# A Conformer block on one core: the eighth chunk's feed-forward products three and five without the columns of its empty rows, and its attention output projected by quarter matrices

## The chip, the cores and the metric

The kernel runs on one core of one Trainium2 chip. The metric is the device time of one execution in microseconds (us), lower is better.

## The reference

The input is `x`, two sequences of 4000 tokens with 512 features, in bfloat16. What is computed, cut to what matters here:

```
h  = layernorm(x);                x1 = x  + 0.5 * silu(h @ w_ff1_a) @ w_ff1_b      # 512 -> 2048 -> 512
h  = layernorm(x1);               x2 = x1 + softmax(h wq (h wk)' * scale) (h wv) @ w_o
h  = layernorm(x2);               conv module: h @ w_pw1, a * sigmoid(b), 3-tap depthwise,
                                  normalised over all tokens, silu(..) @ w_pw2;    x3 = x2 + that
h  = layernorm(x3);               x4 = x3 + 0.5 * silu(h @ w_ff2_a) @ w_ff2_b
return layernorm(x4)
```

## The kernel before

**Chunks and stages.** The tokens are cut into 16 chunks, eight per sequence (`TCB` = 8). A chunk has 512 tokens, four tiles of 128. 4000 is not a multiple of 512: chunk 7 and chunk 15 have 416 tokens, three tiles and 32 tokens over. The 32 tokens left over of both sequences lie in one tile, the fourth tile of chunk 7 (`SHARED`): rows 0 to 31 belong to chunk 7, rows 32 to 63 to chunk 15, rows 64 to 127 hold nothing. So this tile has 64 empty rows of 128. The feed-forward stages handle it with chunk 7; in attention chunk 7 has 416 queries. The stages follow one another: the first feed-forward stage over all chunks, attention over all chunks with the conv module beside it, the second feed-forward stage over all chunks.

**Products by quarters.** Most matrix products use Strassen's scheme in its Winograd form: the two factors are cut into quarters, sums and differences of quarters are formed on VectorE, and seven products of quarters take the place of eight. In `ff_quad` (line 1545) the tokens of a chunk are cut into two halves of two tiles, the features into two halves, the outputs into even and odd blocks. `product(k)` (line 1571) issues one of the seven: four matmuls, each 128x128 weights by a moving matrix of 256 columns, of tiles 0 and 1 or of tiles 2 and 3. Products 1, 2, 6, 7 and 4 go into columns of which tiles 0 and 1 need a part. Products 3 and 5 go only into outputs of tiles 2 and 3. Steps a to d of a quad issue products 1 and 5, 2 and 6, 7 and 3, and 4; between them ScalarE copies (`act(h...)`, `act(m5...)`) and VectorE adds (`plus`) carry sums from one PSUM bank to another. A chunk has four quads, and in between stand the units of the second matrix of the chunk before (`ff_units`).

**Attention output.** While chunk g's attention runs, chunk g-1's is finished in `units_late` (line 2406), step by step of g's 32 key tiles (`kt`). For a chunk of 512 tokens (`whole`) `project_quad` (line 2662) multiplies the 512x512 matrix `Wvo` in quarters: `out_sums` forms four sums of the attention output `OT` on VectorE, then follow 7 products of 4 matmuls with 256 columns, two copies on ScalarE, two additions and eight `residual` operations of 256 columns on VectorE; `project_fetch` brings two sums of weights back from DRAM at `kt` 2 and 6. For chunk 7 `project` (line 2615) does it plainly: for each tile four matmuls of 512 columns, and one `residual` of 512 columns. The weights (stationary) are there the tokens, so the fourth tile, with 32 tokens, uses 32 of the 128 columns of the array. As `Wvo` is kept with one of its quarters replaced by a difference, `project_fetch(3)` brings the true quarter at `kt` 3 and `project_fetch(2)` the difference at `kt` 15.

**The order of the work.** All operations of the program are recorded first, and the class `Plan` (line 112) then sets the order on every engine by a list schedule with its own estimates of durations, looking 60 us ahead, and lets some operations (`either`) go to ScalarE or VectorE. So a change in one place may move rows at others. Since all instructions are issued by the recorder, nearly all have line 95 (L95) in the profile; they are told apart by the tiles that they write and read. Names in the rows: `s` and `y` are the eight PSUM banks, `work`, `sums`, `keys`, `wff` and `xt` are five regions of SBUF, in which the same bytes have several uses over time.

Of the kernel before, what the change touches and what calls it, by code (L numbers as in the profile page):

```python
# [8 lines left out]
ALU = mybir.AluOpType  # L9
AF = mybir.ActivationFunctionType  # L10
# [5 lines left out]
TILE = 128  # L16
TPC = 4
CHUNK = TPC * TILE
N = B * T
TCB = -(-T // CHUNK)  # L20
# [4 lines left out]
SHARED = TCB * TPC - 1  # L25
HALF = 32
# [3 lines left out]
HC, HD, HF = CHUNK // 2, D // 2, FC // 2  # L30
# [11 lines left out]
def width(c):  # L42

    return CHUNK if c % TCB < TCB - 1 else T - (TCB - 1) * CHUNK


def token_tiles(c):

    return TPC if c < NCK - 1 else TPC - 1
# [6 lines left out]
def tile_rows(c, ti):  # L56

    if c % TCB < TCB - 1 or ti < TPC - 1:
        return slice(0, TILE)
    lo = c // TCB * HALF  # L60
    return slice(lo, lo + TAIL)
# [50 lines left out]
class Plan:  # L112
# [49 lines left out]
    @staticmethod  # L162
    def form(call):

        w = call.args[1]
        return tuple(32 if n <= 32 else 64 if n <= 64 else 128 for n in (w.shape[0], Plan.size(w)))
# [431 lines left out]
class Conformer:  # L598
# [564 lines left out]

    def ln_norm(self, c, sl, ti, out, b_out, eng, src=None):
        x, b_x = self.tokens(c, ti, src)
        ways = {"DVE": lambda e: e.tensor_scalar(out, x, self.mv[sl][:, ti, 0:1], self.rs[sl][:, ti:ti + 1], ALU.subtract, ALU.mult),
                "ACT": lambda e: e.activation(out, x, AF.Identity, bias=self.sh[sl][:, ti:ti + 1], scale=self.rs[sl][:, ti:ti + 1])}
        if eng == "any":
            self.S.either(ways, [b_x, self.b_mv[sl][ti], self.b_rs[sl][ti], self.b_sh[sl][ti]], [b_out])
        elif eng == "DVE":  # L1170
            self.S.op("DVE", ways["DVE"], reads=[b_x, self.b_mv[sl][ti], self.b_rs[sl][ti]], writes=[b_out])
        else:
            self.act(out, x, AF.Identity, [b_x, self.b_sh[sl][ti], self.b_rs[sl][ti]], [b_out],
                     bias=self.sh[sl][:, ti:ti + 1], scale=self.rs[sl][:, ti:ti + 1])

    def ln_middle(self, sl, two):
        self.S.op("POOL", lambda e: e.tensor_scalar(self.mv[sl][:, two, 0], self.st[sl][:, two, 0], -1.0 / D, None, ALU.mult),
# [40 lines left out]
    def ln_job(self, c, kind, eng="DVE", plan=(1, 1, 2, 2, 3, 4, 5, 5, 6, 6), slot=None, pe=None):  # L1218

        sl = self.nxt("ln", self.LN_SLOTS)  # L1220
        n = token_tiles(c) if slot is None else TPC
        stats, aggr, shift, norm = plan[0:4], plan[4], plan[5], plan[6:10]

        def tile(ti):
            if kind == "key":
                k = self.keys_home(c)
                self.ln_norm(c, sl, ti, self.h2[k][ti][0:TILE, :], self.b_h2[k][ti], eng)
                if ti == n - 1:
                    self.store_keys(c)
                return  # L1230
            if kind == "out":
                g = c * TPC + ti
                self.ln_norm(c, sl, ti, self.XT[g], self.bx[g], eng)
                if ti == n - 1:
                    self.store_out(c, 0, TPC)
                return
            s = slot if slot is not None else c % 2
            tok, b_tok = self.ltm[ti], self.b_ltm[ti]
            feat, b_feat = self.lnT[s][:, ti], self.b_lnT[s][ti]
            self.ln_norm(c, sl, ti, tok[0:TILE, :], b_tok, eng)  # L1240
            if pe:
                self.after(4, lambda: self.transpose_pe(ti, s, pe[ti], self.bank(4 + ti)))
            else:
                self.transpose(feat, tok, [b_tok], [b_feat])

        for ti in range(n):
            self.after(stats[ti], lambda ti=ti: self.ln_stats(c, sl, ti))
        self.after(aggr, lambda: self.ln_aggr(sl, n))
        if eng == "ACT":
            self.after(shift, lambda: self.ln_shift(sl, n))  # L1250
        for ti in range(n):
            self.after(norm[ti], lambda ti=ti: tile(ti))
# [292 lines left out]
    def ff_quad(self, c, q, st):  # L1545

        S, s = self.S, c % 2
# [7 lines left out]
        n, hw = (3, 3 * 64) if short else (2, HC)  # L1555
# [13 lines left out]

        def product(k, ps, b_ps, start=False):  # L1570
            form, b_f, mv, b_m = forms[k]
            for u in range(2):
                out = ps[:, u * hw:(u + 1) * hw].rearrange("p (t k) -> p t k", t=n)
                for j in range(2):
                    self.mm(out, form(2 * q + u, j), mv[j], start and u == 0 and j == 0, u == 1 and j == 1,
                            b_f + b_m, b_ps, skip_group_check=True)

        def silu(src, b_src, odd, half):
            if short:
# [826 lines left out]
    def units_late(self, o, kt):  # L2406

        if kt == 0:
            self.late_first(o)
        elif kt == 1:  # L2410
            self.late_second(o)
        elif kt < 7:
            m = (kt - 2) * 6
            self.late_third(o, 2, range(m, min(m + 6, PAIRS)))
            self.late_third(o, 4, {3: range(1), 4: range(1, 3), 5: range(3, 9), 6: range(9, PAIRS)}.get(kt, ()))
        whole = width(o) == CHUNK
        if kt == 2:
            self.ln_conv = self.nxt("ln", self.LN_SLOTS)
        if kt in (2, 6) and whole:
            self.project_fetch(kt // 4)  # L2420
        if kt in (3, 15) and not whole:
            self.project_fetch(3 if kt == 3 else 2)
        if kt == 14 and o == NCK - 2:
            self.project_fetch(3)
        if kt == 6 and whole:
            for q in range(2):
                self.S.op("POOL", lambda e, q=q: e.memset(self.OT[0:1, ONES // 128, q * HC:(q + 1) * HC], 0.0),
                          writes=[self.b_OTq[q][ONES // 128]])
            for n in range(4):
                self.out_sums(n)  # L2430
        for n in {7: (0,), 8: (1, 2), 9: (3,)}.get(kt, ()) if whole else ():
            self.project_quad(o, self.ln_conv, n)
        for ti in {9: (0, 1), 13: (2, 3)}.get(kt, ()) if not whole else ():
            self.project(o, ti, self.ln_conv)
            if ti % 2:
                self.ln_middle(self.ln_conv, slice(ti - 1, ti + 1))

    def units(self, g, kt):

# [222 lines left out]
    def project_quad(self, g, sl, step):  # L2662

        S, s = self.S, g % 2
# [4 lines left out]
        form = lambda m: (lambda u, j: self.OS[m][:, j, u * TILE:(u + 1) * TILE], lambda j: self.b_OS[m])  # L2669
        w = lambda k, e: (lambda j: self.Wvo[:, 2 * k + j, e * HD:(e + 1) * HD], self.b_Wvo)  # L2670
        t = lambda m: (lambda j: self.TW[m][:, j], self.b_TW[m])
# [13 lines left out]
        def residual(src, b_src, f, e):  # L2685
            for u in range(2):
                ti = 2 * f + u
                y, b_y = self.XT[g * TPC + ti][:, e * HD:(e + 1) * HD], self.bx[g * TPC + ti]
                S.op("DVE", lambda eng, y=y, u=u, ti=ti: eng.scalar_tensor_tensor(
                    out=y, in0=src[:, u * HD:(u + 1) * HD], scalar=self.rl[s][:, ti:ti + 1], in1=y, op0=ALU.mult, op1=ALU.add,  # L2690
                    accum_out=self.st[sl][:, ti, 2 * e:2 * e + 1]),
                    reads=[b_src, self.b_rl[s], b_y], writes=[b_y, self.b_st[sl][ti]])

        if step == 0:
            product(1, c, b_c, True)
            n = width(g - 1)
            if n < CHUNK:
                self.mm(h[:, n:], self.Wvo[:, 0, 0:128], self.Wvo[:, 0, 0:CHUNK - n], False, True, [self.b_Wvo], b_h,
                        skip_group_check=True)
            self.act(h[:, :], c[:, :], AF.Copy, [b_c], [b_h])  # L2700
            product(5, x, b_x, True)
            self.act(m5, x[:, :], AF.Copy, [b_x], [b_m5])
        elif step == 1:
            product(6, h, b_h)
            plus(x[:, :], b_x)
            product(2, c, b_c)
            residual(c, b_c, 0, 0)
        elif step == 2:
            product(7, h, b_h)
            plus(m5, b_m5)  # L2710
            product(3, x, b_x)
            residual(x, b_x, 0, 1)
            residual(m5, b_m5, 1, 1)
        else:
            product(4, h, b_h)
            residual(h, b_h, 1, 0)
            for k in range(2):
                two = slice(2 * k, 2 * k + 2)
                S.op("POOL", lambda e, two=two: e.tensor_tensor(out=self.st[sl][:, two, 0], in0=self.st[sl][:, two, 0],
                                                                in1=self.st[sl][:, two, 2], op=ALU.add),  # L2720
                     reads=self.b_st[sl][two], writes=self.b_st[sl][two])
                self.ln_middle(sl, two)
# [814 lines left out]
```

## Time and profile before

| what | value |
|---|---|
| median of 3 runs (lowest, highest) | 1843.19 us (1842.84, 1844.6) |
| the profiled execution's own time | 1841.62 us |
| its span, first to last instruction | 1837.5 us |
| busy: TensorE (PE), VectorE (DVE), ScalarE (ACT), GpSimd (POOL) | 1819.4, 1527.7, 1385.4, 159.7 us |
| first feed-forward stage, chunk 7's quads | from 177 to 204 us |
| attention of chunk 8, with chunk 7's projection | from 872 to 932 us |
| second feed-forward stage, chunk 7's quads | from 1580 to 1608 us |

PE, DVE, ACT and POOL are the engines; PEld is the load of TensorE's weights, which runs beside its matmuls; SPq is the queue from which most transfers are issued. In a row of the timeline stand the start, the length until the last of its instructions has ended, the engine, the operation, output and inputs, the shape of the weights and of the moving matrix, how many instructions follow one another, and in brackets the idle time of the engine before them with the engine that ended it. The records of matmuls overlap: the profile draws each until its result has drained, so the time that one costs is the distance between two starts. Some matmul records are missing.

### The profile page before, as it was taken

What the parts mean: (1) busy time and instruction counts of PE and PEld (TensorE: products, weight loads), DVE (VectorE), ACT (ScalarE), POOL (GpSimd) and SP (SyncE); (2) the same over time, 40 slices, a digit from 0 to 9 for tenths busy, and PEclk for the clock granted to TensorE, in tenths of its full rate; (3) what the DMA queues carried; (4) which work ended last, traced back from release to release, by engine and by line L of the source; (5) the groups of instructions that cost most, each with busy time, mean ns of one, the idle gap of its engine ahead of it and who ended that gap; (6) DMA issues with size and microseconds to landing.
All of it is one profiled execution on the core that took longest, in us unless ns stands there. A gap on an engine that the chain in (4) does not pass through costs nothing.

```text
span 1837.5 us, 41511 instructions
## 1 busy us (share of the span) xinstructions
PE 1819.4 (99%) x16279; PEld 1538.7 (84%) x16338; DVE 1527.7 (83%) x3433; ACT 1385.4 (75%) x2468; POOL 159.7 (9%) x413
## 2 busy tenths in 40 slices
PE   9999999999999999999999999999999999999998
PEld 6888888866888888888888888888876888888887
DVE  8888888868777888788877887887888989889886
ACT  5777777755666877787778877887768787787775
POOL 2000000000000010000000000101011000000000
PEclk9999999999999999999999999999999999999999
DMA  7333344297745755558944444544465222221111
GB/s 189 84 88 89 88 99 110 73 259 212 206 139 145 191 169 144 150 156 198 260 114 146 127 130 118 150 126 121 142 209 172 68 70 75 58 64 52 49 44 45
DMA packets 322446, 235.71 MB, mean 128 GB/s; under 512 B 190962, under 2 KB 293045, under 8 KB 321988
## 3 DMA queue, kind: packets, MB, share of 16 engines
q1 hardware_dynamic: 321716, 232.73, 45.5%
q8 instruction: 130, 2.13, 0.5%
q14 instruction: 72, 0.59, 0.1%
q10 hardware_dynamic: 528, 0.26, 0.0%
HBM read 135.22 MB, written 56.74 MB: 104 GB/s over the span
## 4 chain that ended last, share of the span: by engine, by line
PE 95%; DVE 3%; ACT 1%; issue 1%; DMA 0%; POOL 0%; SPq 0%; DVEq 0%
PE y L95 52%; PE s L95 43%; DVE work L95 1%; DVE sums L95 1%; DVE xt L95 0%; ACT sums L95 0%; DVE keys L95 0%; DMA xt<-in_x_dram 0%; DVE wff L95 0%; DVE s L95 0%; POOL work L95 0%; ACT work L95 0%; ACT keys L95 0%; ACT s L95 0%; SPq L95 0%
## 5 line engine op out<-in xcount | busy, mean ns | idle before, releaser
L95 ACT ACTIVATE sums<-s 128x512 bf16<-128x512 f32 (+4 forms) x498 | 291.4, 586 | 137.8 <-PE s L95 133.5
L95 ACT ACTIVATE keys<-s 128x512 bf16<-128x512 f32 (+3 forms) x277 | 158.0, 573 | 138.3 <-PE s L95 109.2
L95 PE MATMUL y<-work,keys 128*128 128x256 bf16 x1920 | 244.3, 273 | 0.3 <-DVE work L95 0.3
L95 DVE TENSOR_TENSOR sums<-sums 128x512 bf16<-128x512 bf16 (+3 forms) x528 | 200.3, 399 | 45.0 <-ACT sums L95 33.1
L95 PE MATMUL y<-sums,keys 128*128 128x256 bf16 (+1 forms) x1440 | 215.1, 270 | 0.0
L95 PE MATMUL s<-sums 128*128 128x256 bf16 (+1 forms) x1428 | 212.6, 272 | 0.0
L95 PE MATMUL y<-wff,keys 128*128 128x256 bf16 (+2 forms) x1590 | 208.9, 276 | 0.4 <-DVE keys L95 0.3
L95 PEld LDWEIGHTS y<-work,keys 128*128 128x128 bf16 x1920 | 187.6, 98 | 23.4 <-DVE work L95 0.6
L95 ACT ACTIVATE work<-xt,work 128x512 bf16<-128x512 bf16 x262 | 202.3, 785 | 6.5 <-DVE work L95 5.7
L95 PE MATMUL y<-work,wff 128*128 128x256 bf16 (+3 forms) x1380 | 205.7, 272 | 0.0
L95 PE MATMUL s<-work,keys 128*128 128x256 bf16 (+4 forms) x1328 | 185.3, 275 | 2.0 <-ACT wff L95 0.6
L95 DVE TENSOR_TENSOR keys<-keys 128x1024 bf16<-128x1024 bf16 (+2 forms) x264 | 168.2, 658 | 10.0 <-ACT keys L95 3.7
L95 PEld LDWEIGHTS y<-wff,keys 128*128 128x128 bf16 (+1 forms) x1592 | 151.0, 98 | 30.0 <-issue 3.0
L95 POOL TENSOR_TENSOR work<-work 128x4 f32<-128x4 f32 (+3 forms) x136 | 101.6, 747 | 851.0 <-DVE work L95 767.4
L95 DVE BATCH_NORM_STATS2 work<-xt 128x6 f32<-128x512 bf16 x251 | 163.1, 680 | 2.0 <-DMA xt<-in_x_dram 1.6
L95 PEld LDWEIGHTS s<-sums 128*128 128x128 bf16 x1428 | 139.0, 98 | 21.7 <-DVE s L95 0.2
L95 PEld LDWEIGHTS y<-sums,keys 128*128 128x128 bf16 x1440 | 138.6, 98 | 17.5 <-issue 0.2
L95 PEld LDWEIGHTS y<-work,wff 128*128 128x128 bf16 x1380 | 133.0, 98 | 17.5 <-DVE wff L95 0.2
L95 PE MATMUL s<-xt,keys 128*128 128x256 bf16 (+1 forms) x924 | 142.4, 270 | 0.5 <-DVE s L95 0.2
L95 PE MATMUL y<-sums,xt 128*128 128x256 bf16 (+1 forms) x960 | 136.4, 270 | 0.4 <-DVE xt L95 0.4
L95 PEld LDWEIGHTS s<-work,keys 128*128 128x128 bf16 (+1 forms) x1348 | 108.9, 97 | 30.6 <-issue 2.3
L95 PE MATMUL s<-xt 128*128 128x256 bf16 (+1 forms) x893 | 133.3, 270 | 0.6 <-ACT s L95 0.6
(171 smaller groups left out, 3432.1 us busy)
## 6 DMA issues: line engine op xcount, KB each, us to landing
xt<-kfd SPq DMA_DIRECT2D x98, 384.0 KB, 3.2
xt<-v12d SPq DMA_DIRECT2D x105, 256.0 KB, 2.9
xd<-xt SPq DMA_DIRECT2D x28, 512.0 KB, 3.6
xt<-xd SPq DMA_DIRECT2D x28, 512.0 KB, 3.7
out_dram<-xt SPq DMA_DIRECT2D x14, 512.0 KB, 2.9
xt<-in_x_dram SPq DMA_DIRECT2D x13, 512.0 KB, 4.2
dcvd<-wff SPq DMA_DIRECT2D x48, 128.0 KB, 3.2
keys<-dcvd SPq DMA_DIRECT2D x12, 512.0 KB, 3.9
```

The costliest lines, as they stand in the source:

```text
L95: return getattr(eng, self.name)(*self.args, **self.kw)
```

## The change

It has two parts.

1. In `product` of `ff_quad`, products 3 and 5 of chunk 7 are issued in two parts for each matmul: 128 columns for tile 2 and 64 columns for tile 3, instead of 256. This holds in both feed-forward stages. `ln_norm` normalises only the 64 filled rows of that tile.
2. Chunk 7's attention output goes through `project_quad` like that of whole chunks. The plain branch, and the two fetches that exchange `Wvo`'s quarter for it, are gone from `units_late`. `residual` is restricted to the rows that belong to the chunk, and the matmul of 96 columns that fills the unwritten end of a bank, issued until now for chunk 8, is issued for chunk 7 too.

```
 class Conformer: ff_quad
         def product(k, ps, b_ps, start=False):
             form, b_f, mv, b_m = forms[k]
+            parts = [(slice(0, n), slice(0, hw // n))]
+            if c == TCB - 1 and k in (3, 5):
+                parts = [(slice(0, 1), slice(0, TILE)), (slice(1, 2), slice(0, 2 * HALF))]
             for u in range(2):
                 out = ps[:, u * hw:(u + 1) * hw].rearrange("p (t k) -> p t k", t=n)
                 for j in range(2):
-                    self.mm(out, form(2 * q + u, j), mv[j], start and u == 0 and j == 0, u == 1 and j == 1,
-                            b_f + b_m, b_ps, skip_group_check=True)
+                    for i, (t, r) in enumerate(parts):
+                        self.mm(out[:, t, r], form(2 * q + u, j), mv[j][:, t, r], start and u == 0 and j == 0 and i == 0,
+                                u == 1 and j == 1 and i == len(parts) - 1, b_f + b_m, b_ps, skip_group_check=True)
...
 ln_job
+            rows = 2 * HALF if slot is None and c * TPC + ti == SHARED else TILE
-            self.ln_norm(c, sl, ti, tok[0:TILE, :], b_tok, eng)
+            self.ln_norm(c, sl, ti, tok[0:rows, :], b_tok, eng)
...
 units_late
-        whole = width(o) == CHUNK
-        if kt in (2, 6) and whole:
+        if kt in (2, 6):
             self.project_fetch(kt // 4)
-        if kt in (3, 15) and not whole:
-            self.project_fetch(3 if kt == 3 else 2)
-        if kt == 6 and whole:
+        if kt == 6:
...
-        for n in {7: (0,), 8: (1, 2), 9: (3,)}.get(kt, ()) if whole else ():
+        for n in {7: (0,), 8: (1, 2), 9: (3,)}.get(kt, ()):
             self.project_quad(o, self.ln_conv, n)
-        for ti in {9: (0, 1), 13: (2, 3)}.get(kt, ()) if not whole else ():
-            self.project(o, ti, self.ln_conv)
-            if ti % 2:
-                self.ln_middle(self.ln_conv, slice(ti - 1, ti + 1))
...
 project_quad, residual
+                r = tile_rows(g, ti)
-                    out=y, in0=src[:, u * HD:(u + 1) * HD], scalar=self.rl[s][:, ti:ti + 1], in1=y, op0=ALU.mult, op1=ALU.add,
-                    accum_out=self.st[sl][:, ti, 2 * e:2 * e + 1]),
+                    out=y, in0=src[r, u * HD:(u + 1) * HD], scalar=self.rl[s][r, ti:ti + 1], in1=y, op0=ALU.mult, op1=ALU.add,
+                    accum_out=self.st[sl][r, ti, 2 * e:2 * e + 1]),
...
 project_quad, step 0
-            n = width(g - 1)
+            n = min(width(g - 1), width(g))
```

What this does to the order of instructions is shown at three places. The first is TensorE in chunk 7 of the first feed-forward stage, where step a of the second quad begins; `s3` is the bank of product 5, `y2` that of product 1, and the rows with `keys` are units of the chunk before. Lines with - are before, with + now.

```order
 L95 MATMUL s0<-sums,wff 128x256 x4
 L95 MATMUL y2<-work,wff 128x256 x4
-L95 MATMUL s3<-sums 128x256 x4
+L95 MATMUL s3<-sums 128x128
+L95 MATMUL s3<-sums 128x64
+L95 MATMUL s3<-sums 128x128
+L95 MATMUL s3<-sums 128x64
+L95 MATMUL s3<-sums 128x128
+L95 MATMUL s3<-sums 128x64
+L95 MATMUL s3<-sums 128x128
+L95 MATMUL s3<-sums 128x64
 L95 MATMUL y1<-work,keys 128x256 x8
```

Four matmuls became eight at the same place; the same stands at product 3 and in the other quads, and apart from that TensorE's order in both feed-forward stages is as before.

The second place is TensorE in the attention of chunk 8. Before, this is the plain projection of chunk 7's third and fourth tile (`s0<-work`, and `s1<-work` with 32 columns of weights) between scores (`s`, `keys`) and products with the values (`sums`).

```order
L95 MATMUL s2<-xt,keys 128x256 x4
L95 MATMUL y2<-sums,keys 128x256 x4
L95 MATMUL s0<-work 128x512 x4
L95 MATMUL y0<-sums,keys 128x256 x4
L95 MATMUL s3<-sums,keys 128x256 x4
L95 MATMUL s1<-work 32x512 x4
L95 MATMUL s0<-work,keys 128x256 x4
```

Now the projection by quarters stands somewhat earlier, at the place of the first two tiles: the fill of 96 columns, then products 5 and 1 and further ones (`s3`, `y3` and `y2` with `work` or `wff`), with conv products (`y0`, `y1`) and scores between.

```order
L95 MATMUL y2<-work 128x96
L95 MATMUL s3<-sums,wff 128x256 x4
L95 MATMUL y0<-work,wff 128x256 x4
L95 MATMUL y1<-work 128x256 x4
L95 MATMUL y3<-work 128x256 x4
L95 MATMUL s2<-xt,keys 128x256 x4
L95 MATMUL y0<-work,wff 128x256 x4
L95 MATMUL s1<-work,xt 128x256 x4
L95 MATMUL y2<-work,wff 128x256 x4
L95 MATMUL y3<-work 128x256 x4
L95 MATMUL y0<-sums,keys 128x256 x6
L95 MATMUL s3<-work,wff 128x256 x4
```

The group with 32 columns of weights is gone, and the rows of scores and values around it, from chunk 7's end to the beginning of chunk 9, are dealt out differently.

The third place is VectorE beside it. Before: the inverse of the softmax sums, then the residuals of the first two tiles one by one, with sums of keys (`keys<-keys`, `xt`) and of probabilities (`sums<-sums`) between.

```order
L95 TENSOR_TENSOR keys<-keys 128x2x2x128
L95 RECIPROCAL work<-work 128x4
L95 TENSOR_TENSOR sums<-keys 32x256
L95 SCALAR_TENSOR_TENSOR xt,work<-s0,work,xt 128x512
L95 TENSOR_TENSOR sums<-keys 128x256
L95 SCALAR_TENSOR_TENSOR xt,work<-s1,work,xt 128x512
L95 TENSOR_TENSOR sums<-sums 128x512 x2
L95 TENSOR_TENSOR xt<-keys 128x512
```

Now the two additions of `plus` and the eight residuals stand nearly in one piece, and sums of probabilities and keys wait behind them.

```order
L95 TENSOR_TENSOR s3<-y2,work 128x512
L95 TENSOR_TENSOR work<-work 128x2x256
L95 TENSOR_TENSOR xt<-s2,xt 128x512
L95 SCALAR_TENSOR_TENSOR xt,work<-y3,work,xt 128x256
L95 TENSOR_TENSOR work<-y2,work 128x512
L95 SCALAR_TENSOR_TENSOR xt,work<-y3,work,xt 128x256
L95 SCALAR_TENSOR_TENSOR xt,work<-s3,work,xt 128x256
L95 SCALAR_TENSOR_TENSOR xt,work<-work,xt 128x256
L95 SCALAR_TENSOR_TENSOR xt,work<-s3,work,xt 128x256
L95 SCALAR_TENSOR_TENSOR xt,work<-work,xt 32x256
L95 SCALAR_TENSOR_TENSOR xt,work<-y2,work,xt 128x256
L95 SCALAR_TENSOR_TENSOR xt,work<-y2,work,xt 32x256
```

Ten operations of VectorE stand where two did, and the sums of the next pairs of key tiles begin after the last of them.

More of the change, by code (lines that the diff above doesn't have):

```diff
@@ L1165, in ln_norm @@
         x, b_x = self.tokens(c, ti, src)
-        ways = {"DVE": lambda e: e.tensor_scalar(out, x, self.mv[sl][:, ti, 0:1], self.rs[sl][:, ti:ti + 1], ALU.subtract, ALU.mult),
-                "ACT": lambda e: e.activation(out, x, AF.Identity, bias=self.sh[sl][:, ti:ti + 1], scale=self.rs[sl][:, ti:ti + 1])}
+        n = out.shape[0]
+        x, mean, rs, sh = x[0:n], self.mv[sl][0:n, ti, 0:1], self.rs[sl][0:n, ti:ti + 1], self.sh[sl][0:n, ti:ti + 1]
+        ways = {"DVE": lambda e: e.tensor_scalar(out, x, mean, rs, ALU.subtract, ALU.mult),
+                "ACT": lambda e: e.activation(out, x, AF.Identity, bias=sh, scale=rs)}
         if eng == "any":
@@ L1172, in ln_norm @@
         else:
-            self.act(out, x, AF.Identity, [b_x, self.b_sh[sl][ti], self.b_rs[sl][ti]], [b_out],
-                     bias=self.sh[sl][:, ti:ti + 1], scale=self.rs[sl][:, ti:ti + 1])
+            self.act(out, x, AF.Identity, [b_x, self.b_sh[sl][ti], self.b_rs[sl][ti]], [b_out], bias=sh, scale=rs)
     def ln_middle(self, sl, two):
@@ L2687, in residual @@
                 ti = 2 * f + u
-                y, b_y = self.XT[g * TPC + ti][:, e * HD:(e + 1) * HD], self.bx[g * TPC + ti]
-                S.op("DVE", lambda eng, y=y, u=u, ti=ti: eng.scalar_tensor_tensor(
-                    out=y, in0=src[:, u * HD:(u + 1) * HD], scalar=self.rl[s][:, ti:ti + 1], in1=y, op0=ALU.mult, op1=ALU.add,
-                    accum_out=self.st[sl][:, ti, 2 * e:2 * e + 1]),
+                r = tile_rows(g, ti)
+                y, b_y = self.XT[g * TPC + ti][r, e * HD:(e + 1) * HD], self.bx[g * TPC + ti]
+                S.op("DVE", lambda eng, y=y, u=u, ti=ti, r=r: eng.scalar_tensor_tensor(
+                    out=y, in0=src[r, u * HD:(u + 1) * HD], scalar=self.rl[s][r, ti:ti + 1], in1=y, op0=ALU.mult, op1=ALU.add,
+                    accum_out=self.st[sl][r, ti, 2 * e:2 * e + 1]),
                     reads=[b_src, self.b_rl[s], b_y], writes=[b_y, self.b_st[sl][ti]])
```

## The prediction, made before the changed kernel was run

> **What bounds the kernel now.** I read the page first: the span, the busy times and the chain of work that ended last.
>
> ```profile
> span 1837.5 us, 41511 instructions
> ...
> PE 1819.4 (99%) x16279; PEld 1538.7 (84%) x16338; DVE 1527.7 (83%) x3433; ACT 1385.4 (75%) x2468; POOL 159.7 (9%) x413
> ...
> PE 95%; DVE 3%; ACT 1%; issue 1%; DMA 0%; POOL 0%; SPq 0%; DVEq 0%
> ```
>
> TensorE is busy for 99% of the span and makes up 95% of the chain. So a matmul that gets shorter shortens the kernel, as long as VectorE and ScalarE can follow. Whether they can is read from the stretches that the change touches: chunk 7's quads in both feed-forward stages, and chunk 8's attention. The view of busy times by stretch gives, after the length, PE, PEld, DVE, ACT and POOL, then the granted clock.
>
> ```profile
> 177.00:204.00 27.00, 27.00 (x249) 24.21 (x248) 24.45 (x52) 20.97 (x35) 2.01 (x2) 1.00 0.37 108
> 1580.00:1608.00 28.00, 27.89 (x241) 23.57 (x242) 24.73 (x50) 22.20 (x37) 2.02 (x2) 1.00 0.22 59
> 872.00:932.00 60.00, 58.81 (x534) 49.00 (x539) 53.05 (x128) 47.34 (x87) 4.35 (x15) 1.00 0.87 239
> 880.00:912.00 32.00, 31.90 (x287) 27.13 (x288) 27.84 (x69) 22.18 (x41) 2.72 (x12) 1.00 1.00 260
> 912.00:928.00 16.00, 15.36 (x140) 12.95 (x138) 15.08 (x35) 14.51 (x27) 1.63 (x3) 1.00 0.66 221
> 928.00:936.00 8.00, 7.95 (x70) 6.75 (x70) 7.16 (x19) 6.55 (x12) 0.00 (x0) 1.00 0.73 201
> 936.00:944.00 8.00, 8.00 (x93) 6.43 (x92) 4.76 (x9) 4.58 (x10) 0.00 (x0) 1.00 0.30 92
> ```
>
> Feed-forward: PE full, DVE 24.45 of 27 (91%) and 24.73 of 28 (88%), clock 1.00. Attention of chunk 8: PE loses 1.19 us of 60. From 912 to 928 DVE is busy 15.08 of 16 (94%) and ACT 14.51, and there PE loses 0.64. That is the tight place.
>
> **Part 1, the split products.** What a matmul costs is the distance of starts. The timeline of TensorE in chunk 7's first stage:
>
> ```profile
> 183.05 0.60 PE L95 MATMUL s<-sums 128*128 128x256 bf16 x4
> 183.49 1.04 PE L95 MATMUL y<-work,keys 128*128 128x256 bf16 x8
> 184.36 0.60 PE L95 MATMUL s<-sums 128*128 128x256 bf16 x4
> ```
>
> Product 5 (at 183.05) takes 0.436 us for four matmuls, 109 ns each (eight in 0.87 us give the same). For 128, 96 and 32 columns, all with weights of their own of 128x128:
>
> ```profile
> 8.02 1.05 PE L95 MATMUL s<-work,wff 128*128 128x128 bf16 x16 [0.45 <-ACT work L95]
> 8.91 0.39 PE L95 MATMUL y<-work 128*128 128x128 bf16 x4
> ...
> 939.72 0.26 PE L95 MATMUL y<-work,wff 128*128 128x32 bf16 x4
> ```
> ```profile
> 883.71 0.21 PE L95 MATMUL s<-xt 128*128 128x96 bf16 x1
> 883.75 0.34 PE L95 MATMUL y<-sums,keys 128*128 128x208 bf16 x2
> ```
>
> Sixteen of 128 columns take 0.89 us, 55.6 ns each. One of 96 takes 0.04 us. Four of 32 columns span 0.26 us; a short one drains in 0.18 us, so the three distances are (0.26 - 0.18) / 3, about 27 ns. No row has 64 columns: it lies between 27 and 40 ns, and the slope of 128 to 256 columns (53.4 ns for 128) gives 55.6 - 26.7 = 28.9 ns. I take 29, since 128 and 96 columns lie on that line. A pair costs 55.6 + 29 = 84.6 ns instead of 109, so 24.4 ns are saved. There are 2 stages x 4 quads x 2 products x 4 matmuls = 64 of them: **1.56 us** (0.86 us with 40 ns, 1.69 with 27).
>
> The Trainium skill, TensorE: Matmul & The Clock Gate, section Back-to-back issue gap, speaks against this: a stream of weight loads and matmuls sustains only about 81 ns at 128 columns. With its 25 ns for up to 64 columns (the table there) a pair would cost 106 ns, the split would save 0.2 us, and the time would be 1842.4. The trace disagrees: 55.6 ns at 128 columns, with a load for each.
>
> What follows on the saved 0.1 us of product 5: product 6 (at 184.36) needs ScalarE's copy of product 1.
>
> ```profile
> 183.44 0.58 ACT L95 ACTIVATE s<-y 128x512 f32<-128x512 f32 x1
> ```
>
> It ends at 184.02, 0.34 us before product 6; moved up by 0.1 us, product 6 still finds it ready. So the gain is on the path; without this cover it would be lost, nothing more. DVE's load would rise to 24.45 of 26.2 (93%), still hidden. The normalisation of 64 instead of 128 rows costs the same or less and hides in ACT's 6 idle us of 27.
>
> **Part 2, the projection.** TensorE's rows of the plain one:
>
> ```profile
> 899.32 1.03 PE L95 MATMUL s<-work 128*128 128x512 bf16 x4
> 900.18 0.38 PE L95 MATMUL y<-sums,xt 128*128 128x256 bf16 x2
> ...
> 907.95 0.61 PE L95 MATMUL s<-sums,keys 128*128 128x256 bf16 x4
> 908.49 1.04 PE L95 MATMUL s<-work 128*32 128x512 bf16 x4
> 909.46 0.61 PE L95 MATMUL s<-work,keys 128*128 128x256 bf16 x4
> ```
>
> A tile takes 0.86 us, four take 3.44. The last one uses 32 columns of the array, and the change of form costs on both sides: 0.54 us for four matmuls of 0.436 ahead of it (0.10), and 0.97 for 0.86 in it (0.11). Together 3.65 us. By quarters: 28 matmuls of 109 ns, 3.05 us, and the fill of 96 columns 0.04, together 3.09. TensorE saves **0.56 us**.
>
> VectorE gets more. The same steps one chunk later, and the plain residual:
>
> ```profile
> 960.02 0.42 DVE L95 TENSOR_TENSOR work<-work 128x512 bf16<-128x512 bf16 x1
> 960.36 0.42 DVE L95 TENSOR_TENSOR wff<-work,wff 128x512 bf16<-128x512 bf16 x1
> ...
> 961.45 0.70 DVE L95 TENSOR_TENSOR s<-y,work 128x512 f32<-128x512 f32 x1
> 962.05 0.48 DVE L95 SCALAR_TENSOR_TENSOR xt<-y,work,xt 128x256 bf16<-128x256 f32 x1
> 962.45 0.08 DVE L95 DVE_READ_ACCUMULATOR xt<-y,work,xt 128x1 f32 x1
> ```
> ```profile
> 900.39 0.75 DVE L95 SCALAR_TENSOR_TENSOR xt<-s,work,xt 128x512 bf16<-128x512 f32 x1
> 901.06 0.08 DVE L95 DVE_READ_ACCUMULATOR xt<-s,work,xt 128x1 f32 x1
> ```
>
> By starts: 4 sums of 0.34, 2 additions of 0.60, 8 residuals of 0.40 make 5.76 us; 4 residuals of 0.67 go (2.68). Net **+3.08 us of DVE**. ScalarE gets two copies, about 1.2 us. POOL gets two fills and two small additions and is 93% idle there. SP issues two fetches of 128 KB instead of two: the exchanged quarter's at steps 3 and 15 go, those of two sums at 2 and 6 come, earlier than their products. The first residual waits, as before, for the inverse of the softmax sums, which comes through DRAM; sums of probabilities and keys are queued behind it on DVE, and the next scores and value products wait for those. From 880 to 936 us DVE has 50.08 of 56; with 3.08 more it has 53.2 of 55.4 (96%), but 3.2 us of room follow from 936 to 944. So I take the DVE work as hidden, at its edge, with the waits there neither better nor worse.
>
> **The sum.** 1.56 + 0.56 = 2.12 us less. The profiled execution took 1841.62, 4.1 more than its span, so 1839.5; its own time is 1.57 below the median shown, from which the forecast is 1843.19 - 2.12 = **1841.1 us**.
>
> **The rivals.**
>
> Waits that vanish. Around chunk 7's end and in chunk 8 PE waits for ACT and DVE; from 850 to 930 us the view of waits has:
>
> ```profile
> PE s L95 <- ACT s L95: 1.1, 3, 0.4
> PE s L95 <- DVE sums L95: 0.4, 1, 0.4
> PE s L95 <- DVE s L95: 0.4, 2, 0.2
> ```
>
> That is 1.9 us in six waits, and as a drawn matmul ends some 0.16 us after the next could start, each costs that much more: 2.9 us. The order of just these rows is new, and some conv work of ScalarE moves from the full stretch before 875 to the emptier one behind it. If this removes most of them, 1838.2 to 1839.8, say 1839.0. Against it: DVE gets more work, not less.
>
> Slower: VectorE becomes the bound of chunk 8. The price is its 3.1 us, if none finds room: 1841.1 + 3.1 = 1844.2, 1.0 above the time before. It decides the sign once more than 2.12 us of it comes to light as waits of PE. For it: at 94% DVE load PE loses 4% (912 to 928), and the ten operations in one piece hold up sums for 4.4 us. Against it: 88% to 91% in the feed-forward stretches cost next to nothing.
>
> Slower by more: the loads of weights are not hidden behind short matmuls.
>
> ```profile
> L95 PEld LDWEIGHTS s<-sums 128*128 128x128 bf16 x1428 | 139.0, 98 | 21.7 <-DVE s L95 0.2
> ```
>
> If each had to end before the next matmul, a pair would cost 196 ns instead of 109: 64 x 87 ns = 5.6 us, 1841.1 + 1.6 + 5.6 = 1848.2. The rows of 27 and 55.6 ns exclude it unless a change of length costs something of its own.
>
> The split does nothing, because loads and short matmuls together take as long as the 256 columns did: 1843.19 - 0.56 = 1842.6. No row has such pairs alternating in length, which is for it; the rows above, with equal lengths, are against it. The Trainium skill's rule, quoted above, would put the time near this case.
>
> **How the numbers follow.** The sum as it stands 0.5 (its own range 1840.0 to 1842.2, from 27 and 40 ns and half a microsecond of waits either way), vanishing waits 0.23, VectorE as bound 0.17, split without gain 0.06, loads not hidden 0.04. The range takes in most of the second and third case: 1838.4 to 1844.2; outside are the end of the second, the last and what I overlooked. A measurement of this kernel tells about 0.2%, 3.7 us, from no change, so faster means below 1839.5: most of the second case, 0.17. Slower, above 1846.9: the loads, and VectorE with waits that add up beyond its own work, 0.07. Within: 0.76.
>
> **What would show it.** Distances of starts in products 3 and 5 of 56 and 29 ns, and no new wait of PE from 177 to 204 and from 1580 to 1608 us, would show part 1 right. For part 2 the group 128*32 is gone, PE from 872 to the start of chunk 9's attention has 0.56 us less to do, and its waits for DVE and ACT between 850 and 944 stay near 1.9 us. Waits of 4 us or more there would make the forecast wrong on the slow side, below 0.5 us on the fast side; a pair at 109 ns or more would prove part 1 wrong.

## The result, and the profile after

The kernel after takes **1840.72 us** (median of 22 runs, 1838.89 to 1843.55), the kernel before, run beside it, 1843.30 us (median of 22 runs, 1841.32 to 1844.92). The ratio is 0.9987, with a 95% interval from 0.9981 to 0.9993: 2.4 us less, between 1.3 and 3.5. The prediction said 1841.1 us, 2.1 less than before, in a range from 1838.4 to 1844.2.

The page of the profile after, with the lines that answer to those of before:

```profile
span 1836.8 us, 41748 instructions
...
PE 1819.5 (99%) x16415; PEld 1538.9 (84%) x16415; DVE 1530.3 (83%) x3447; ACT 1389.0 (76%) x2470; POOL 163.8 (9%) x417
...
PE 94%; DVE 4%; ACT 1%; DMA 1%; issue 0%; POOL 0%; SPq 0%; DVEq 0%
```

TensorE (PE) is still the bound. VectorE (DVE) is busy for 2.6 us more, ScalarE (ACT) for 3.6. This span is only 0.7 us shorter than that of before; why a single pair of spans misleads here is told below.

Chunk 7's quads in the first feed-forward stage, on TensorE. Eight matmuls in one row are four pairs of 128 and 64 columns; the row that follows tells when they were over.

```profile
182.81 0.50 PE L95 MATMUL s<-sums 128*128 128x128 bf16 x8
183.15 1.04 PE L95 MATMUL y<-work,keys 128*128 128x256 bf16 x8
184.02 0.60 PE L95 MATMUL s<-sums 128*128 128x256 bf16 x4
```
```profile
183.20 0.58 ACT L95 ACTIVATE s<-y 128x512 f32<-128x512 f32 x1
```

Four pairs take 0.34 us, 85 ns each. Over all split products of the trace, the distance from 128 columns to the next start is 56 to 57 ns, and from 64 columns 28 ns. Product 6 (at 184.02) finds ScalarE's copy of product 1 ready, as that ends at 183.78. The view of busy times by stretch shows what this does to the engines (length; then PE, PEld, DVE, ACT, POOL; then the granted clock):

```profile
177.00:204.00 27.00, 27.00 (x289) 24.47 (x287) 24.10 (x53) 21.61 (x37) 2.01 (x2) 1.00 0.38 118
1578.00:1606.00 28.00, 28.00 (x277) 23.80 (x276) 24.74 (x50) 22.42 (x37) 2.02 (x2) 1.00 0.25 58
872.00:932.00 60.00, 59.35 (x563) 51.42 (x561) 55.08 (x139) 48.41 (x89) 4.83 (x19) 1.00 1.00 237
...
912.00:928.00 16.00, 15.72 (x145) 13.72 (x143) 14.39 (x35) 14.78 (x25) 0.58 (x2) 1.00 0.94 267
```

PE stays full in both feed-forward stretches. In chunk 8's attention DVE rises from 53.05 to 55.08 us of 60, and PE does not fall but rises from 58.81 to 59.35. The waits of TensorE from 850 to 944 us, in the view of waits (in all, times, longest):

```profile
PE s L95 <- ACT s L95: 1.4, 2, 1.1
PE s L95 <- DVE sums L95: 0.6, 2, 0.4
```

The sum is 2.0 us, as before (1.9), but in four waits instead of six. The view counts a wait only from the drawn end of the matmul ahead of it, some 0.16 us after the next could have started. So the sharper measure is the distance of starts less what the columns take, wherever that is over 0.1 us and no record is missing: 3.4 us from 845 to 950 before and 2.9 after. This is called the loss below.

**Where the time went.** The start of the same matmul in both traces gives the time lost or won in each stretch. The stretches are named by the times of before. The single profiled executions give, in us against before (a negative number is time won):

| kernel | chunk 7, first stage (177 to 205) | 850 to 949 | 949 to 1325 | 1325 to 1392 | 1392 to 1403 | chunk 7, second stage (1578 to 1699) |
|---|---|---|---|---|---|---|
| after | -0.77 | -1.16 | -0.37 | +2.25 | 0.00 | -0.77 |
| split alone | -0.77 | -0.01 | +0.16 | +0.53 | +1.67 | -0.78 |
| projection alone | 0.00 | -1.18 | -0.38 | +0.82 | +1.66 | 0.00 |
| plain, last tile in the full array | 0.00 | -1.03 | -0.67 | +0.01 | 0.00 | 0.00 |
| quads sooner | -0.77 | -1.18 | -0.66 | +1.46 | 0.00 | -0.77 |
| quads later | -0.78 | -0.34 | -0.69 | +1.00 | 0.00 | -0.77 |
| more VectorE work in chunk 8 | -0.78 | +1.97 | -0.35 | +0.46 | +1.67 | -0.77 |

The lower six rows are experiments told below. The first, second, third and last columns of numbers repeat from kernel to kernel within 0.2 us wherever the program is the same. The fourth and fifth do not, although the edits lie elsewhere.

In the fifth, the granted clock differs. The stretches of the split alone, and then of before (the column after POOL is the clock):

```profile
1394.00:1396.00 2.00, 0.93 (x11) 0.89 (x11) 1.32 (x4) 1.82 (x5) 0.00 (x0) 0.84 1.13 325
1396.00:1398.00 2.00, 2.00 (x11) 1.40 (x10) 1.90 (x5) 1.57 (x4) 0.00 (x0) 0.50 1.11 372
1398.00:1400.00 2.00, 1.96 (x11) 1.20 (x10) 1.32 (x4) 0.60 (x2) 0.00 (x0) 0.81 0.97 320
```
```profile
1394.00:1396.00 2.00, 1.90 (x22) 1.79 (x23) 1.44 (x4) 1.89 (x5) 0.00 (x0) 1.00 1.11 347
1396.00:1398.00 2.00, 1.95 (x12) 1.04 (x11) 2.00 (x5) 1.71 (x5) 0.00 (x0) 1.00 1.00 356
1398.00:1400.00 2.00, 2.00 (x13) 1.11 (x12) 1.95 (x4) 2.00 (x4) 0.00 (x0) 1.00 0.55 215
```

Three of the fourteen profiled executions have this dip. The lost clock is 0.16, 0.50 and 0.19 of 2 us, together 1.7 us, or 3.4 us at half rate. In the fourth column a wait for a DMA stands, in the kernel after until 1335.69 us:

```profile
PE y L95 <- DMA xt<-v12d: 1.7, 1, 1.7
```

The wait is absent in the trace of before and 0.4 us long in that of the split alone. (The rest of the fourth column is a gap of 0.3 us near 1371, which the order of some kernels has.) A pair of traces may thus be off by 2 us for reasons that have nothing to do with a change, and the times of one kernel spread by 2.5 to 4.7 us wherever there were ten runs or more. The first three columns of the table and the last are free of it.

### The profile page after: what moved, and what is told of

It reads as the page before. It is cut to its first block, busy times and chain, and to the rows that moved or that the text cites. A ratio compares the mean times of both kernels' runs of the same rounds, so it can differ in the third digit from the quotient of the medians.

```text
span 1836.8 us, 41748 instructions
## 1 busy us (share of the span) xinstructions
PE 1819.5 (99%) x16415; PEld 1538.9 (84%) x16415; DVE 1530.3 (83%) x3447; ACT 1389.0 (76%) x2470; POOL 163.8 (9%) x417
## 4 chain that ended last, share of the span: by engine, by line
PE 94%; DVE 4%; ACT 1%; DMA 1%; issue 0%; POOL 0%; SPq 0%; DVEq 0%
PE y L95 52%; PE s L95 42%; DVE work L95 1%; DVE sums L95 1%; DVE xt L95 1%; DVE wff L95 0%; ACT sums L95 0%; DVE keys L95 0%; DMA xt<-v12d 0%; DMA xt<-in_x_dram 0%; ACT work L95 0%; DVE s L95 0%; POOL work L95 0%; ACT keys L95 0%; SPq L95 0%
## 5 line engine op out<-in xcount | busy, mean ns | idle before, releaser
L95 PE MATMUL s<-sums 128*128 128x256 bf16 (+2 forms) x1460 | 211.9, 269 | 0.0
L95 PE MATMUL y<-wff,keys 128*128 128x256 bf16 (+3 forms) x1592 | 209.3, 276 | 0.2 <-DVE keys L95 0.2
L95 ACT ACTIVATE work<-xt,work 128x512 bf16<-128x512 bf16 (+1 forms) x262 | 202.0, 786 | 5.9 <-DVE work L95 5.5
L95 PE MATMUL s<-work,keys 128*128 128x256 bf16 (+4 forms) x1348 | 189.3, 276 | 1.8 <-ACT s L95 1.4
```

The costliest lines, as they stand in the source:

```text
L95: return getattr(eng, self.name)(*self.args, **self.kw)
```

## The experiments

### The split alone

The kernel before with the hunks of `ff_quad` and `ln_norm` only.

> The kernel before with part 1 alone (products 3 and 5 of chunk 7 in 128 and 64 columns, normalisation of 64 rows). My theory: 64 matmuls save 24.4 ns each, so about 1.5 us less than before (0.9 to 1.7), half of it in each stage, with starts 56 and 29 ns apart and no new wait. Rival, the split gains nothing because loads and short matmuls take as long as the 256 columns did: 0 us. Rival, loads not hidden: 5.6 us more.

1841.33 us against 1843.17 (ratio 0.9991, 0.9982 to 1.0000): 1.7 us less, between 0 and 3.3. In the trace it is 0.77 us in the first stage and 0.78 in the second, 1.55 together, with nothing lost in between. My theory holds. The first rival, no gain at all, sits at the edge of the interval, but the trace excludes it; the second is out by 7 us.

### The split in all quads, with all columns

The kernel after, but with the split in nearly all quads; outside chunk 7 no column is left out. The 856 split matmuls show the price of splitting without its gain.

```
-            if c == TCB - 1 and k in (3, 5):
-                parts = [(slice(0, 1), slice(0, TILE)), (slice(1, 2), slice(0, 2 * HALF))]
+            if not short and k in (3, 5):
+                parts = [(slice(0, 1), slice(0, TILE)), (slice(1, 2), slice(0, 2 * HALF if c == TCB - 1 else TILE))]
```

> The kernel after with products 3 and 5 split in every quad by quarters of both feed-forward stages; outside chunk 7 nothing is dropped, 128 and 128 columns stand for 256. That is 107 quads x 8 = 856 matmuls more. My theory, a split costs only 2 x 55.6 - 109 = 2.2 ns: 1.9 us more than after, 0.7 us less than before. Rival, loads not hidden behind short matmuls: 856 x 87 ns = 74 us more.

1842.88 us against 1842.62 beside it (ratio 0.9999, 0.9989 to 1.0009), so 2.2 us more than after by the ratios, with some 2 us either way; 1.9 were expected. The trace is sharper: the splits outside chunk 7 cost 1.0 us in each feed-forward stage, 2.4 ns each. In the timeline of chunk 8's quads in the first stage eight matmuls of 128 columns take 0.44 us:

```profile
208.99 0.61 PE L95 MATMUL s<-work,sums 128*128 128x128 bf16 x8
209.43 1.04 PE L95 MATMUL y<-work,keys 128*128 128x256 bf16 x8
```

That is 55 ns for each, with weights of its own for each. Loads stay hidden. The page TensorE: Matmul & The Clock Gate of the Trainium skill, section Back-to-back issue gap, gives 81 ns for a stream of loads and matmuls at 128 columns. An estimate by that page is 856 x (162 - 109) ns = 45 us for the splits; the trace and the time disagree with it.

### The split in all quads, 64 columns dropped

```
-            if c == TCB - 1 and k in (3, 5):
+            if not short and k in (3, 5):
```

> The kernel after with 128 and 64 columns in products 3 and 5 of every quad by quarters, not of chunk 7 alone; it leaves out half of the fourth tile in these two products. 856 matmuls more save 24.4 ns each. If TensorE stays the bound: 20.9 us less than after, about 23.5 less than before. Rival, VectorE (about 90% busy there) or ScalarE cannot follow: 10 us less than after or still smaller a gain, with new waits of TensorE in the quads.

1819.42 us against 1842.62 (ratio 0.9873, 0.9856 to 0.9889): 23.2 us less than before by the medians, where 23.5 were expected. The view by stretch, first of this kernel, then of after:

```profile
60.00:340.00 280.00, 280.00 (x3029) 253.85 (x3027) 253.18 (x530) 224.76 (x379) 27.50 (x23) 1.00 0.36 95
```
```profile
60.00:340.00 280.00, 280.00 (x2608) 250.75 (x2607) 247.59 (x514) 220.72 (x368) 26.19 (x23) 1.00 0.35 93
```

PE is full over these 280 us in both, and DVE only rises from 88% to 90%, since a shorter PE stage draws its other work together. The term of 24.4 ns a pair is confirmed at 14 times the size of the change, and the cover by VectorE with it.

### The projection alone

The kernel before with the hunks of `units_late` and `project_quad` only.

> The kernel before with part 2 alone (chunk 7's attention output projected by quarters). The sum of the prediction: 0.56 us less than before, with TensorE's loss to waits between 850 and 944 us near that of before (3.2 us counted as distances of starts beyond the columns). The traces of before and after differ there by 1.15 us, so a second theory is that the new order also takes away about 0.6 us of waits: 1.1 us less, loss near 2.7 us. Rival, VectorE as the bound of chunk 8: 1 to 2.6 us more than before, loss of 5 us or more there. The times can tell the third from the other two; the first two are told apart by the loss alone.

1841.16 us against 1843.17 (ratio 0.9993, 0.9984 to 1.0002): 1.3 us less by the ratio, between 2.9 less and 0.4 more. The loss is 2.9 us from 845 to 950, after 3.4 before. From 850 to 944, where I had given my figures, it is 2.9 after 3.2, so between the 2.7 and the 3.2 of the two theories. What favours the second is the table: -1.18, where it wanted 1.1 less, and another -0.38 in the chunks behind. VectorE as the bound is out: it wanted 5 us of loss.

### The plain projection in the full array

The kernel before; only the last tile's matmuls use 128 tokens as weights instead of 32. Nothing else of part 2 is in it.

```
-        n, t0 = r.stop, ti * TILE - r.start
+        n, t0 = TILE if g == TCB - 1 else r.stop, ti * TILE - r.start
```

> The kernel before; the plain projection of chunk 7's fourth tile uses 128 columns of the array instead of 32 (the other 96 outputs are not used). If the change of form costs 0.10 us ahead and 0.11 us in it: the four matmuls ahead of it take 0.44 us from start to start, not 0.54, and the four 0.86, not 0.97. If the extra time had another cause, it stays.

The eight matmuls of the last two tiles now stand in one piece (the rows are from a second profile of the same kernel; in the first, one of the eight records is missing):

```profile
905.91 1.89 PE L95 MATMUL s<-work 128*128 128x512 bf16 x8
907.63 0.60 PE L95 MATMUL y<-sums,xt 128*128 128x256 bf16 x4
```

From start to start it is 1.72 us for eight, 0.86 for four, against 0.97 and another 0.10 ahead of it in the kernel before. The change of form did cost 0.21 us. The one run took 1840.21 us, 2.4 below the median of the runs of before beside it, which the 0.21 do not explain. Eleven runs of the same kernel follow.

> The kernel before with the fourth tile's plain projection in 128 columns of the array, now timed; the look at it showed 1840.21 us in one run, 2.4 below the runs of before beside it. From its trace: 0.2 us less for the change of form and 0.5 us less of waits between 845 and 950 us, so 0.7 us less than before. If the one run was typical: 2 us or more less than before, and the projection by quarters has then no part in the gain.

1840.31 us against 1842.98 (ratio 0.9989, 0.9980 to 0.9998): 2.0 us less, between 0.4 and 3.7. The trace has 1.03 us in chunk 8 and 0.67 in the chunks behind it. The loss from 845 to 950 is 2.7 us, 0.7 less than before. The waits from 850 to 944 are much those of the kernel after:

```profile
PE s L95 <- ACT s L95: 1.4, 2, 1.1
PE s L95 <- DVE sums L95: 0.6, 1, 0.6
```

So in the traces **this edit of one number gains at least what all of part 2 gains**: 1.70 us, where the projection alone has 1.56, less 0.3 near 1371. The times, 2.0 and 1.3 us, don't tell the two apart. The planner counts 95 ns for each change of form (`CHANGE`); without the narrow tile it arrives at another order, which loses less in chunk 8, and later chunks take less time too. But the second reading goes too far where it leaves the projection by quarters no part: from 845 to 950 its matmuls have 0.35 us less of columns to do, with the fill counted, and this edit saves none.

### The order of the projection

The kernel after, with other steps for chunk 7's projection.

```
-        for n in {7: (0,), 8: (1, 2), 9: (3,)}.get(kt, ()):
+        for n in ({7: (0, 1), 8: (2,), 9: (3,)} if o == TCB - 1 else {7: (0,), 8: (1, 2), 9: (3,)}).get(kt, ()):
```

> The kernel after; in chunk 8's attention steps 0 and 1 of the projection by quarters are both recorded at key tile 7, step 2 at 8, step 3 at 9 (after: 0 at 7, 1 and 2 at 8, 3 at 9). Same work in another order. If the waits around the projection are an accident of the order: TensorE's loss between 845 and 950 us (2.9 us in the kernel after, as distances of starts beyond the columns) moves by 0.5 us or more in either direction and the time with it. If they belong to the work: within 0.3 us of after.

1839.21 us against 1842.98 (ratio 0.9980, 0.9971 to 0.9989). The loss from 845 to 950 stays at 2.9 us; the stretch behind it gains 0.3 us more than in the kernel after. It is the fastest of the kernels that leave out nothing, though its interval overlaps that of after.

> As the run before, but step 0 at key tile 7, step 1 at 8, steps 2 and 3 at 9. Same two theories: the loss between 845 and 950 us moves by 0.5 us or more from 2.9 with the order, or stays within 0.3.

1839.97 us against 1842.98 (ratio 0.9985, 0.9976 to 0.9994). Here the loss is 3.75 us, 0.8 more, and the table's second stretch shows just that (-0.34 for -1.16). So one of the two orders moved the waits by more than the whole 0.56 us that part 2 saves on TensorE, and the other left them. The waits depend on the order. The totals can't tell this: by the ratios the time of this kernel is not above that of after, and the intervals overlap.

### The projection by quarters, undone in all chunks

```
-        whole = width(o) == CHUNK
+        whole = False
...
-        if kt in (3, 15) and not whole:
+        if kt in (3, 15) and (o < NCK - 2 or kt == 3):
             self.project_fetch(3 if kt == 3 else 2)
-        if kt == 14 and o == NCK - 2:
-            self.project_fetch(3)
```

> The kernel before with the plain projection in all 15 chunks that are projected beside attention, not in chunk 7 alone: part 2 undone fourteen times. If TensorE's work alone counts, each of 14 chunks costs 16 x 215 ns = 3.44 us instead of 28 x 109 = 3.05, together 5.4 us more than before. Rival, VectorE's load limits attention: its 3.1 us less in each of 14 chunks gives time back, so the kernel is no slower than before, or faster.

1848.56 us against 1843.17 (ratio 1.0030, 1.0018 to 1.0042): 5.4 us more by the medians, between 3.3 and 7.7 by the ratio; TensorE's own difference of 0.39 us in 14 chunks makes 5.4 too. That the two agree to the digit is luck: the pair of traces has 6.5. The page of this kernel:

```profile
PE 1823.5 (99%) x16081; PEld 1518.2 (82%) x16168; DVE 1488.0 (81%) x3237; ACT 1371.3 (74%) x2440; POOL 142.1 (8%) x357
```

VectorE's busy time falls from 1527.7 to 1488.0 us, and nothing comes back for it. The rival, VectorE's load as a limit, is out.

### More work for VectorE ahead of the projection

In the first kernel only beside chunk 8's attention, in the second in all chunks (with `True` for the condition).

```
-            for n in range(4):
+            for n in ((0, 1, 2) * 4 + (3,) if o == TCB - 1 else range(4)):
                 self.out_sums(n)
```

> The kernel after; in chunk 8's attention the first three sums of the attention output are formed four times instead of once (same values), nine operations of 0.34 us, 3.1 us more of VectorE just where part 2 put its 3.1 us. If VectorE's work there is hidden: 0 to 0.5 us more than after, so 2.1 to 2.6 us less than before. If VectorE is at its limit there: about 3 us more than after, so 0.5 us more than before, with new waits of TensorE for VectorE between 850 and 944 us.

1842.56 us against 1843.17 (ratio 0.9998, 0.9989 to 1.0007), so 2.0 us more than after by the ratios. The trace has 3.1 us more than after from 850 to 949 (+1.97 for -1.16), the full length of the nine operations. So the price that the rival asked for part 2 is paid for this work. But the waits are mostly not those for VectorE that I expected; the new ones are:

```profile
893.15 0.21 PE L95 MATMUL y<-work 128*128 128x96 bf16 x1
894.05 0.61 PE L95 MATMUL y<-work 128*128 128x256 bf16 x4 [0.70 <-ACT wff L95]
895.34 0.61 PE L95 MATMUL y<-work 128*128 128x256 bf16 x4 [0.67 <-ACT y L95]
...
899.12 0.60 PE L95 MATMUL y<-work,wff 128*128 128x256 bf16 x4 [0.25 <-DVE wff L95]
```

> The kernel after; the first three sums of the attention output are formed four times (same values) in all 15 chunks projected beside attention: 15 x 3.1 = 46 us more of VectorE, 5% of its load in each chunk. If that is hidden behind TensorE: up to 3 us more than after (chunk 8's share included). If VectorE's pieces hold up TensorE wherever they stand: 0.5 us or more in each chunk, 8 to 46 us more than after.

1878.51 us against 1842.62 (ratio 1.0196, 1.0179 to 1.0213): 38 us more than after, 2.5 in each of 15 chunks, though VectorE was busy for only 83% there (450 to 1350 us). My reading of cover by load is wrong here. Twelve of the chunks have the same two waits. TensorE's timeline in one of them, this kernel first, then after:

```profile
537.77 0.60 PE L95 MATMUL y<-work,wff 128*128 128x256 bf16 x4
539.11 0.61 PE L95 MATMUL y<-work 128*128 128x256 bf16 x4 [0.74 <-ACT wff L95]
540.46 0.61 PE L95 MATMUL y<-work 128*128 128x256 bf16 x4 [0.73 <-ACT y L95]
540.99 0.61 PE L95 MATMUL y<-work,wff 128*128 128x256 bf16 x4
541.44 0.60 PE L95 MATMUL y<-work 128*128 128x256 bf16 x4
```
```profile
534.51 0.60 PE L95 MATMUL y<-work,wff 128*128 128x256 bf16 x4
534.95 0.60 PE L95 MATMUL s<-sums,wff 128*128 128x256 bf16 x4
535.39 0.60 PE L95 MATMUL y<-work,wff 128*128 128x256 bf16 x4
535.83 1.04 PE L95 MATMUL y<-work 128*128 128x256 bf16 x8
536.70 0.60 PE L95 MATMUL s<-xt,keys 128*128 128x256 bf16 x4
```

After the first row, the next products into the same bank (`y3`, as the kernel has it) need ScalarE's copy of it. Its rows in this kernel:

```profile
538.46 0.59 ACT L95 ACTIVATE wff<-y 128x512 f32<-128x512 f32 x1
539.82 0.58 ACT L95 ACTIVATE y<-y 128x512 f32<-128x512 f32 x1 [0.76 <-PE y L95]
```

Each copy starts 0.1 us after the matmuls ahead of it have drained, and the matmuls that wait start 0.06 us after its end. In the kernel after, other products stand between (at 534.95, 535.39 and the first half of 535.83) and fill the time. With the sums late, these come behind it, and TensorE waits for ScalarE twice. In distances of starts that is 0.90 + 0.90 us in this chunk, and 0.23 more ahead of the group at 542.11: 2.0 of some 2.5 us.

### The same work at another place

The kernel after, with nine additions of the same size at step 16, on buffers that nobody needs then.

```
+        if kt == 16:
+            (a, b_a), (x, b_x), (y, b_y) = zip(self.OS, self.b_OS)
+            for _ in range(9):
+                self.S.op("DVE", lambda e: e.tensor_tensor(out=a, in0=x, in1=y, op=ALU.add), reads=[b_x, b_y], writes=[b_a])
```

> The kernel after; again nine additions of 0.34 us on VectorE in each of 15 chunks, 46 us in all, but at step 16 of attention and on buffers that nobody waits for then, not ahead of the projection (their results are not used). Where they stood ahead of the projection they cost 37.8 us. If that was VectorE's load, it costs about as much here: 30 to 40 us more than after. If it was their place, ahead of the sums for which the projection's products wait, it costs next to nothing here: up to 3 us more than after.

1842.36 us against 1842.98 (ratio 0.9995, 0.9986 to 1.0005): 1.5 us more than after by the ratios, where the other place cost 38. The same 60 us, about the length of a whole chunk's attention, with the work elsewhere and then with the work ahead of the projection:

```profile
630.00:690.00 60.00, 60.00 (x562) 52.26 (x560) 52.12 (x132) 47.86 (x89) 5.06 (x20) 1.00 0.57 169
```
```profile
630.00:690.00 60.00, 58.40 (x541) 49.64 (x540) 51.51 (x129) 46.21 (x84) 3.77 (x17) 1.00 0.56 164
```

With 52.12 us of VectorE nothing waits, with 51.51 us PE loses 1.6. So the place makes the price, not the load.

## Why the prediction was right, point by point

**TensorE bounds the kernel.** Right. Columns taken away or added came out of the time at their full length, in three kernels: 23.2 us of 23.5, and within some 2 us either way 5.4 of 5.4 and 2.2 of 1.9.

**Part 1, 1.56 us.** Right in mechanism and size: 1.54 us in the trace of after, 1.55 in that of the split alone. The two ends of the unknown 64 columns, 27 and 40 ns, close at 28. The cover held: product 6 met a copy that was ready 0.24 us earlier. The two rivals on this part are out, by the trace more than by the times.

**Part 2, TensorE 0.56 us.** The single terms are right: the change of form measures 0.21 us, and 0.39 us a whole chunk for the columns is confirmed by 14 chunks. But the step "with the waits there neither better nor worse" failed, on the good side. From 850 to 949 us the kernel gains 1.16 us, 0.56 from this term and about 0.45 from fewer waits; the rest are distances too small to count singly. The sign that I had named, the view of waits, hides this (2.0 for 1.9 us). Another 0.37 us comes in the chunks behind, of which I had said nothing. Against that stands a new gap of 0.3 us near 1371, which the projection alone has too and the two other orders have not.

**Vanishing waits.** This rival named the mechanism, a new order, but expected from it 1.3 to 2.9 us of gain beyond the forecast; it came to about half a microsecond. The runs show that it isn't owed to the projection by quarters: the plain one without the narrow tile has it too.

**VectorE hidden, at its edge.** The verdict was right, and the argument behind it wrong. I weighed VectorE's load, 96% of a stretch. What counts is whether work stands ahead of the sums for which the projection waits. 3.1 us more at that place cost 3.1 us in the trace; 3.1 us in each chunk elsewhere cost 0.1. Part 2's own 3.1 us measure 3.0 in the projection alone. ScalarE was taken too low, 1.2 us for the two copies, where the projection alone has 3.0 more; where the rest comes from was not traced.

**The sum.** 2.12 us against 2.4 (1.3 to 3.5). Without the stretch of random events, the trace of after has 0.77 + 1.16 + 0.37 + 0.77 = 3.07, less 0.3 at 1371, so 2.7 us. The term that was too small is that of waits in chunk 8 and behind it, taken as zero, worth about 0.6. That the time came out within 0.4 us of the forecast is partly luck, since its interval is 2.2 us wide and the times alone could not have told 2.1 from 2.7.

**What stays open.** Why the later chunks gain 0.35 to 0.69 us in six kernels, beyond the fact that their order differs, was not traced wait by wait. That it is the counted 95 ns that make the planner choose another order was not tried by itself. And the sooner order's lead over after isn't settled, since their intervals overlap.

## What to carry to other kernels

A matmul over columns that nobody reads can be cut even where it makes two instructions of one, if a row of the trace shows that starts at the shorter length follow at that length; here 128 + 64 columns took 85 ns instead of 109. Extra work on an engine with room to spare is free or costs up to its full length, according to what stands behind it: look for the chain that it lengthens before the load. Where a planner sets the order, a gain of half a microsecond may be the order's and not the edit's; a kernel that changes little but the planner's input, as the one with the full array did, tells which.

## What was not expected of the hardware

The granted clock falls to half for 3.4 us at about 1395 us in three of fourteen profiled executions, and costs 1.7 us. Ahead of it TensorE waits 0.83, 0.72, 0.43 and 1.23 us within 9 us, as distances of starts, in executions with and without the dip alike. What differs is where a fixed grid falls: in the clock records of all fourteen traces the clock changes only at whole multiples of 3.413 us after it first was full, and that moment lies elsewhere in each execution. In the three with the dip the last three waits fall into one stretch of the grid, which loses 2.3 to 2.4 us, and the dip is the stretch behind it. No stretch of the other eleven traces loses more than 2.0 us from that moment to the program's end. So short waits that add up within one stretch bring the dip, and the limit lies between 2.0 and 2.3 us of 3.4, as far as fourteen traces and one place tell.

The Trainium skill, TensorE: Matmul & The Clock Gate, Part 1 on the clock gate, states that the clock follows how busy TensorE was in a window of 3413 ns that runs freely and does not restart with the kernel; the length and the changing phase agree. The Trainium skill, TensorE: Matmul & The Clock Gate, section HAM oscillation, gives the rule to avoid idle gaps of over 3.4 us; here the longest gap is 1.2 us, so the rule is too weak for this kernel.

A wait for the same DMA (`xt` from `v12d`, at 1335 us) was 0.3, 1.5 and 1.7 us long in three traces (projection alone, split in all quads with all columns, after) whose instructions have the same order there, and 0 and 0.4 us in another two (before, split alone). Together the two events can be larger than the change itself.
